# Keys and values of tile pairs in seven block products, and fp32 state and numerators on tiles of the array

## The chip, the core and the metric

The kernel runs on one core of one Trainium2 chip. The metric is the time of one execution on the device in microseconds (us). TensorE (PE) multiplies matrices into PSUM, ScalarE (ACT), VectorE (DVE) and GpSimd (POOL) do the elementwise work, and SyncE (SP) issues most transfers.

## The reference

One layer for 2048 tokens of width 512, all in fp32:

```python
xn = layernorm(x)
q, k, v = split(xn @ wqkv)                     # 32 heads of 16
pq = einsum("bhsd,hdf->bhsf", q, w_phi)        # the same for pk
phi_q = concat([softmax(pq), softmax(-pq)])    # 32 features a head; the same for phi_k
kv = einsum("bhsf,bhsd->bhfd", phi_k, v)       # the state
z = einsum("bhsf->bhf", phi_k)
num = einsum("bhqf,bhfd->bhqd", phi_q, kv)     # the numerators
den = einsum("bhqf,bhf->bhq", phi_q, z)[..., None] + 1e-6
s = reshape(num / den) @ wo
gate, up = xn @ W_gate, xn @ W_up              # 512 to 1376
g = silu((gate * (gate > 0) * up) @ W_down)
out = x + s * g
```

The state is summed over all tokens, so no numerator can be formed before the last token's keys and values are there.

## The kernel before

**Precision.** Large products run in the rounded format fp32r, one pass each. An operand is split into a high part (rounded copy, ScalarE) and a low part (the rest, VectorE or GpSimd), and a product takes three matmuls: low by high, high by low, high by high. `mm3` issues them. A matmul of plain fp32 operands appears in the trace as two records.

**Tile stage.** The tokens come as 16 tiles of 128, in an order (`order`) that alternates between two blocks of 512, so that tiles 2m and 2m+1 are the same columns of two blocks. For each tile: normalisation (`norm_stats`, `norm_scale`, `norm_apply`), four transposes into `pxT`, the high and low parts of the turned tile into `XT`, and for each pair the sums of blocks that a Strassen-Winograd scheme needs (`sums_x`, `sums_hi`, `sums_lo`; the slots of `XT` are A11, A12, A21, A22 and S1 to S4). The feed-forward part uses these sums: `gate_up` has seven block products instead of eight. Keys and values do not: `project` takes 12 matmuls of 512 columns for `pk` (keys, with `w_phi` folded into the weights) and 12 for `pv`, per tile. `query` takes 12 more per tile (`pq`) and stores the result. `exponents` subtracts maximum and minimum per head on VectorE, `exp_part` is on ScalarE, `features` normalises, `features_split` makes the features' high and low part (`phl`) and adds the features to `zacc` with an accumulating transfer on GpSimd's queue. `kv_products` takes 8 matmuls of 256 columns per tile into four banks (`pkv`): high and low part of the values by high and low part of the features.

**State.** `state` adds the parts, transposes 32 by 32 blocks, and builds `kvhl`, block-diagonal 128 by 128 weights in a high and a low part. `zB` holds the sums of the features.

**Feed-forward part.** Two halves of 1024 tokens. In each, 11 slices of 128 hidden columns: `gate_up` (7 blocks of 6 matmuls of 512 columns), and `down` for groups of slices (`py`). In the first half the weight slices are combined and split by `f_prep` and stored, in the second half they are reloaded (`f_reload`). Slices 2 and 3 (`AHEAD`) are prepared and stored during the tile stage already, and reloaded in the first half too. At the end of each half `out_tile` multiplies by `wo` (`pso`).

**Queries' back part.** Beside it, eight units (`UNITS`, each two tiles of 128 by 1024 features) go through `q_pair` (exponents, weights, normalisation) and then `q_back` or `q_back2`: transpose, a high part on ScalarE, a low part on VectorE or GpSimd, and products with `kvhl` into `pnum`: 16 matmuls of 256 columns (`q_back`, two units) or 8 of 512 (`q_back2`, six units). The result is stored in two parts to DRAM (`o_store`), one is loaded and the other added to it by an accumulating transfer (`o_sum`), and `o_split` prepares it for `wo`.

**Order.** The program order of each engine is the order of issue. A planner (`Clock`) keeps an estimate of each engine's time from a table of costs; side work (weight preparation, units, stores) is a set of generators that `pump` advances when their engine is estimated to be nearly free and their inputs ready. `finish` forces the rest. `START`, `LEAD`, `LATER` and `DOWNS` are due places set by hand. All operations are recorded at one line, L59, so groups of the profile are told apart by their tiles.

Of the kernel before, what the change touches and what calls it, by code (L numbers as in the profile page):

```python
# [28 lines left out]
B8, B4, B2 = 3, 8, 41  # L29
# [6 lines left out]
AHEAD = (2, 3)  # L36

LATER = 9
START = (12, 15)
# [3 lines left out]
A21, A22, A11, A12, S1, S2, S3, S4 = range(8)  # L43
# [19 lines left out]
class Clock:  # L63
# [21 lines left out]
    def issued(self, key, name, a, k):  # L85
# [9 lines left out]
        if key == "tensor":  # L95
            n = o.free_size()
            cost = max(n, 245) + 30
            if name == "matmul" and a[2].dtype == F32 and not k.get("is_transpose"):
                cost = n * 3 + 460
# [60 lines left out]
def layer_kernel(ctx: ExitStack, tc: tile.TileContext, x, wkT, wqT, wv, wo, wf, cst, out):  # L160
# [93 lines left out]
    mhalf = sb.tile([P, 96], F32, name="mhalf")[:, 0:1]  # L254
# [4 lines left out]
    def norm_stats(n):  # L259
        xt = X.pop(n)  # L260
        xn = u2((P, D), "xn")
        sm, ss, rs, bias = small(1, "lm"), small(1, "lv"), small(1, "lr"), small(1, "lb")
        nc.scalar.activation(xn, xt, AF.Copy, scale=-1.0 / D, accum_out=sm)
        nc.scalar.activation(xn, xt, AF.Square, bias=sm, accum_out=ss)
        XN[n] = xn, xt, bias, rs, sm, ss

    def norm_scale(n):
        xn, xt, bias, rs, sm, ss = XN[n]
        nc.vector.tensor_scalar(rs, ss, 1.0 / D, 1e-5, op0=ALU.mult, op1=ALU.add)
        nc.gpsimd.tensor_tensor(rs, rs, mhalf, op=ALU.pow)  # L270

    def norm_apply(n):
        xn, xt, bias, rs, sm, ss = XN[n]
        nc.vector.tensor_scalar(bias, sm, rs, None, op0=ALU.mult)
        nc.scalar.activation(xn, xt, AF.Identity, bias=bias, scale=rs)
        XN[n] = xn

    def norm_vector(n):

        xt = X.pop(n)  # L280
        st, mv, rs = small(6, "bs", 2), small(2, "bm", 2), small(1, "br", 2)
        nc.vector.bn_stats(st, xt)
        nc.vector.bn_aggr(mv, st)
        nc.vector.tensor_scalar(rs, mv[:, 1:2], 1e-5, None, op0=ALU.add)
        nc.gpsimd.tensor_tensor(rs, rs, mhalf, op=ALU.pow)
        XN[n] = u2((P, D), "xn"), xt, mv, rs

    def norm_vector_apply(n):
        xn, xt, mv, rs = XN[n]
        for c in [slice(0, 256), slice(256, D)] if n == 0 else [slice(0, D)]:  # L290
            nc.vector.tensor_scalar(xn[:, c], xt[:, c], mv[:, 0:1], rs, op0=ALU.subtract, op1=ALU.mult)
        XN[n] = xn
# [27 lines left out]
    def turn(m, full=True):  # L320
        p = transpose_x(m)
        hi_xt(m, p)
        if full:
            full_xt(m, p)
        return m, p

    def sums_x(n):

        x0, x1 = XF.pop(n - 1), XF.pop(n)
        sa, sb_ = u2((P, 2, 2, P), "sa"), u2((P, 2, 2, P), "sb")  # L330
        add(nc.gpsimd, sa[:, 0], x1[:, 0], x1[:, 1])
        add(nc.gpsimd, sb_[:, 0], x0[:, 0], x1[:, 0], ALU.subtract)
        add(nc.gpsimd, sa[:, 1], sa[:, 0], x0[:, 0], ALU.subtract)
        add(nc.gpsimd, sb_[:, 1], x0[:, 1], sa[:, 1], ALU.subtract)
        SF[n] = sa, sb_

    def sums_hi(n):
        for s, c in zip(SF[n], (S1, S3)):
            nc.scalar.activation(XT[:, c:c + 2, 0, :, cols(n)], s, AF.Copy)

    def sums_lo(n):
        for s, c in zip(SF.pop(n), (S1, S3)):
            add(nc.gpsimd, XT[:, c:c + 2, 1, :, cols(n)], s, f32(XT[:, c:c + 2, 0, :, cols(n)]), ALU.subtract)
# [62 lines left out]

    def features(n, e, raised, pv, between):

        vhl = u4((P, H, 2, DH), "vhl", F32R)
        pvg = pv.rearrange("p (h f) -> p h f", f=DH)  # L410
# [3 lines left out]
        nc.scalar.activation(vhl[:, :, 0, :], pvg, AF.Copy)  # L414
# [3 lines left out]
        add(nc.vector, vhl[:, :, 1, :], pvg, f32(vhl[:, :, 0, :]), ALU.subtract)  # L418
        nc.vector.tensor_reduce(sm, groups(e), op=ALU.add, axis=AX.X)
        nc.vector.reciprocal(pv[:, 0:64], sm)  # L420
        VH[n] = vhl
        if n:
            features_scale(n, e, pv)

    def features_scale(n, e, pv):
        phi = e if n else zacc
        nc.vector.tensor_tensor(groups(phi), groups(e), pv[:, 0:64].unsqueeze(2).to_broadcast([P, 64, DH]), op=ALU.mult)
        EK[n] = phi

    def features_split(n):  # L430
        phi = EK.pop(n)
        phl = u8((P, NG, 2, P), "phl", F32R)
        split(phl[:, :, 0, :], phl[:, :, 1, :], flat(phi).rearrange("p (g f) -> p g f", g=NG), nc.gpsimd)
        if n:
            nc.gpsimd.dma_start(zacc, phi, accum_op=ALU.add)
        PHI[n] = phl

    def kv_products(n):
        phl, vhl = PHI.pop(n), VH.pop(n)
        if n == 0:  # L440
            PKV.extend(ps((P, 2, 256), name="pkv") for _ in range(NG // 2))
# [15 lines left out]
    def f_load(f):  # L457
        if f == AHEAD[-1]:
# [21 lines left out]
    def f_prep(f, keep=True):  # L480
# [20 lines left out]
        yield "gpsimd", wa[0]  # L501
        for c in range(2):
            add(nc.gpsimd, wa[1][:, c], rg[c][:, :, 0, :], f32(wa[0][:, c]), ALU.subtract)
# [5 lines left out]
        yield "gpsimd", wb[0]  # L509
        add(nc.gpsimd, wb[1], ta, f32(wb[0]), ALU.subtract)  # L510
# [4 lines left out]
        yield "gpsimd", wc[0]  # L515
        add(nc.gpsimd, wc[1], tb, f32(wc[0]), ALU.subtract)
# [8 lines left out]
        yield "gpsimd", fd[0]  # L525
        add(nc.gpsimd, fd[1], rd, f32(fd[0]), ALU.subtract)
# [180 lines left out]
    def q_pair(u):  # L707
# [87 lines left out]
        BACK[u] = pace.add((q_back if parts[0][0] == parts[1][0] else q_back2)(u, es, ez), first=True)  # L795
# [11 lines left out]
    def od(q):  # L807

        if q not in OD:
            OD[q] = dram((P, 4, 256), f"od{q}"), dram((P, 4, 256), f"ol{q}")  # L810
        return OD[q]

    def turned_parts(u, es, ez, j, pieces):

        th, tl = u4((P, 1024), "pTh", F32R), u4((P, 1024), "pTl", F32R)
        n = 1024 // len(pieces)

        a = 2 if len(pieces) == 2 else 1
        hi, lo = (t.rearrange("p (a t x) -> p t a x", a=a, x=32) for t in (th, tl))

        def blocks(t):
            return t.rearrange("p (t a x) -> p t a x", a=a, x=32)
        if UNITS[u][0][0] in QUERIES[0]:

            ez[j] = None
            for i in range(2):
                e, k = pieces[i * len(pieces) // 2]
                k += i * 512 % n
                et, c = ps(name="peT"), slice(16 // a * i, 16 // a * (i + 1))
                yield "vector", e  # L830
                nc.vector.transpose(et, flat(e)[:, k:k + 512])
                yield "scalar", et
                nc.scalar.activation(hi[:, c], blocks(et), AF.Copy)
                yield "vector", th
                add(nc.vector, lo[:, c], blocks(et), f32(hi[:, c]), ALU.subtract)
        else:
            et = ez[j]
            for i, (e, k) in enumerate(pieces):
                yield "vector", e
                nc.vector.transpose(et[:, i * n:(i + 1) * n], flat(e)[:, k:k + n])  # L840
            yield "scalar", et
            nc.scalar.activation(hi, blocks(et), AF.Copy)
            yield "gpsimd", th
            add(nc.gpsimd, lo, blocks(et), f32(hi), ALU.subtract)
        DONE_Q[u] += 1
        return th, tl

    def q_back(u, es, ez):

        (q, _), _ = UNITS[u]  # L850
        for j in range(2):
            th, tl = yield from turned_parts(u, es, ez, j, [(es[j], 0)])
            ez[j] = None
            yield "tensor", tl
            os_ = flat(es[j]).rearrange("p (a s t) -> p a s t", a=2, s=2)
            vh, vl = (t.rearrange("p (d t a x) -> p d a t x", d=2, a=2, x=32) for t in (th, tl))
            for a in range(2):
                p = ps((P, 2, 256), name="pnum")
                for s in range(2):
                    g = 4 * a + 2 * j + s  # L860
                    o = p[:, s, :].rearrange("p (t x) -> p t x", x=32)
                    mm(o, kvhl[:, 1, g, :], vh[:, s, a], s == 0, False)
                    mm(o, kvhl[:, 0, g, :], vl[:, s, a], False, True)
                nc.scalar.activation(os_[:, a], p, AF.Copy)
            es[j] = None
            del th, tl, vh, vl
            DONE_Q[u] += 1
            STORES[u].append(pace.when(os_, lambda j=j, os_=os_: [o_store(q, j, s, os_[:, :, s, :]) for s in range(2)]))
        yield None,

    def q_back2(u, es, ez):

        (q0, j), (q1, _) = UNITS[u]
        for s in range(2):
            th, tl = yield from turned_parts(u, es, ez, s, [(e, 512 * s) for e in es])
            if s:
                es[:] = [None] * 2
            yield "tensor", tl
            os_ = u4((P, 1024), "os") if ez[s] is None else ez[s]
            ez[s] = None  # L880
            os_ = os_.rearrange("p (a q t) -> p a q t", a=2, q=2)
# [499 lines left out]
```

## Time and profile before

| | |
|---|---|
| Median of 3 runs | 563.15 us (562.89 to 563.59) |
| The profiled execution | 562.88 us, span 561.1 us |
| Records of matmuls | 2618 |
| Mean granted TensorE clock | 1.0 |
| DMA | 137.98 MB, mean 246 GB/s |

The span runs from the first to the last instruction of the core. A matmul's busy time (0.389 us for 512 columns) overlaps that of its neighbours, so durations of a piece of the stream are read from the chain of work that ended last, where each piece lasts until the next begins.

### The profile page before, as it was taken

How to read it: one execution, taken by the hardware profiler on the slowest of the kernel's cores; microseconds unless marked ns; L12 is line 12 of the kernel's file. 1: busy time of each engine (PE TensorE's matmuls, PEld its weight loads, DVE VectorE, ACT ScalarE, POOL GpSimd, SP SyncE). 2: the span in 40 equal slices, each digit the busy share in tenths (PEclk: the TensorE clock that was granted, in tenths of full speed). 3: DMA queues.
4: the chain of work that ended last, by engine and by line, in shares of the span. 5: the costliest groups of instructions: out<-in, count | busy, mean ns of one | idle time of the engine just before them, and what ended most of it. 6: DMA issues, size and time to landing. Idle time of an engine off the chain costs nothing.

```text
span 561.1 us, 8197 instructions
## 1 busy us (share of the span) xinstructions
PE 555.5 (99%) x2618; PEld 465.0 (83%) x2618; DVE 386.2 (69%) x584; ACT 303.1 (54%) x543; POOL 404.6 (72%) x347
## 2 busy tenths in 40 slices
PE   8999999999999999999999999999999999999997
PEld 8888888888888888888888888887888888888886
DVE  5978777676657897799963432799883948665323
ACT  3898687765555557456464151235465555644510
POOL 1689987899888487997978333473568786888473
PEclk9999999999999999999999999999999999999999
DMA  8358999855599817979779999991755765559874
GB/s 285 132 157 238 269 270 324 245 153 166 150 304 321 313 61 261 356 266 285 269 250 322 331 388 410 370 396 47 202 187 193 244 206 183 157 179 320 252 210 165
DMA packets 84539, 137.98 MB, mean 246 GB/s; under 512 B 7824, under 2 KB 34320, under 8 KB 83600
## 3 DMA queue, kind: packets, MB, share of 16 engines
q1 hardware_dynamic: 81040, 125.33, 64.7%
q0 software_dynamic: 3312, 12.06, 11.1%
q8 instruction: 21, 0.34, 0.2%
q14 instruction: 22, 0.18, 0.1%
q10 hardware_dynamic: 144, 0.07, 0.0%
HBM read 76.87 MB, written 52.69 MB: 231 GB/s over the span
## 4 chain that ended last, share of the span: by engine, by line
PE 93%; DVE 3%; DMA 2%; issue 0%; SPq 0%; POOL 0%
PE py L59 21%; PE pd L59 10%; PE pa L59 9%; PE pb L59 8%; PE pv L59 8%; PE pk L59 8%; PE pq L59 8%; PE pso L59 8%; PE pc L59 6%; PE pkv L59 3%; PE pnum L59 3%; PE pxT L59 1%; PE pfold L59 1%; DMA pql<-pq 1%; DMA wd<-ws 1%; DVE eq L59 1%
## 5 line engine op out<-in xcount | busy, mean ns | idle before, releaser
L59 PE MATMUL py<-fdh,hl 128*128 128x512 f32 x176 | 68.5, 389 | 0.0
L59 PE MATMUL py<-fdh,hh 128*128 128x512 f32 x176 | 68.5, 389 | 0.0
L59 PE MATMUL py<-fdl,hh 128*128 128x512 f32 x176 | 68.5, 389 | 0.0
L59 PE MATMUL pa<-XT,wa 128*128 128x512 f32 x264 | 67.0, 389 | 0.0
L59 PEld LDWEIGHTS pa<-XT,wa 128*128 128x128 f32 x264 | 49.6, 188 | 10.3
L59 DVE TENSOR_TENSOR y<-py,y 128x512 f32<-128x512 f32 x40 | 27.5, 689 | 36.5 <-PE py L59 36.5
L59 POOL TENSOR_TENSOR phl<-ek,phl 128x1024 fp32r<-128x1024 f32 x15 | 36.1, 2409 | 10.7 <-ACT phl L59 10.7
L59 PE MATMUL pv<-wvh,XT 128*128 128x512 f32 x128 | 43.5, 401 | 0.0
L59 PE MATMUL pk<-wkh,XT 128*128 128x512 f32 x128 | 42.4, 392 | 0.0
L59 POOL TENSOR_TENSOR ez<-eq,zB 128x1024 f32<-128x1024 f32 x16 | 38.5, 2415 | 4.4 <-ACT eq L59 2.0
L59 POOL TENSOR_TENSOR hl<-t,hh 128x512 fp32r<-128x512 f32 x16 | 20.8, 1298 | 27.3 <-ACT hh L59 26.3
L59 PE MATMUL pq<-XT,wqh 128*128 128x512 f32 (+1 forms) x144 | 40.3, 366 | 0.0
L59 PEld LDWEIGHTS py<-fdh,hh 128*128 128x128 f32 x176 | 33.0, 188 | 6.9
L59 PEld LDWEIGHTS py<-fdl,hh 128*128 128x128 f32 x176 | 33.0, 188 | 6.8
L59 PEld LDWEIGHTS py<-fdh,hl 128*128 128x128 f32 x176 | 33.0, 188 | 6.8
L59 POOL TENSOR_TENSOR y<-y,ys 128x512 f32<-128x512 f32 x24 | 30.9, 1291 | 9.6 <-ACT ys L59 9.6
L59 PE MATMUL pd<-XT,wd 128*128 128x512 f32 x132 | 33.8, 390 | 0.5 <-DVE t L59 0.5
L59 PE MATMUL pd<-XT,wc 128*128 128x512 f32 x132 | 33.8, 389 | 0.0
L59 POOL TENSOR_TENSOR ol<-of,oh 128x512 fp32r<-128x512 f32 (+1 forms) x13 | 20.2, 1596 | 18.9 <-ACT oh L59 18.9
L59 PE MATMUL pc<-XT,wb 128*128 128x512 f32 x132 | 33.7, 389 | 0.0
L59 PE MATMUL pb<-XT,wb 128*128 128x512 f32 x132 | 33.5, 389 | 0.0
L59 POOL TENSOR_TENSOR pTl<-ez,pTh 128x1024 fp32r<-128x1024 f32 x10 | 24.0, 2400 | 8.4 <-ACT pTh L59 8.4
(174 smaller groups left out, 1559.2 us busy)
## 6 DMA issues: line engine op xcount, KB each, us to landing
zacc<-ek POOLq DMA_DIRECT2D x15, 512.0 KB, 5.8
xts<-XT SPq DMA_DIRECT2D x4, 1792.0 KB
XT<-xts SPq DMA_DIRECT2D x7, 1024.0 KB, 20.4
wa<-ws SPq DMA_DIRECT2D x26, 256.0 KB, 3.2
wb<-ws SPq DMA_DIRECT2D x26, 256.0 KB, 4.8
wc<-ws SPq DMA_DIRECT2D x26, 256.0 KB, 5.1
ws<-wa SPq DMA_DIRECT2D x22, 256.0 KB, 4.0
ws<-wb SPq DMA_DIRECT2D x22, 256.0 KB, 4.2
```

The source lines that it names most:

```text
L59: return self.tc.keep_in_program_order(op(*a, **k))
```

## The change

It has three parts.

**Seven products.** From pair 3 on (`FIRST`), the keys and values of tiles 2m and 2m+1 are one product of 2 by 2 blocks, in seven blocks of 6 matmuls with the sums S1 to S4 of the tokens and combined weights `T`. `pair` replaces the loop over single tiles for m of 1 to 7. The combined weights are made in pairs 1 to 3 by 28 steps, placed by hand in `PLAN` (first letter: engine v, g or s; second: combine, high or low). The token sums are made by two differences on VectorE and two additions on GpSimd. The second tile's normalisation statistics go to VectorE from pair 3 on, and one of two feature scalings to GpSimd.

**fp32 on tiles of the array.** `kv_products` multiplies features and values unsplit, 16 matmuls of 64 columns on four 32-column strips, all into one bank. Numerators are 16 matmuls of 256 columns per unit on eight tiles of 64 rows by 32 columns (`q_back` for all units), with `kvt` as 32-column weights. `features_split` splits nothing any more, `turned_parts`, `q_back2`, `o_store` and `o_sum` go, and a unit is stored with two transfers.

**Moves.** `AHEAD` is empty: slices 2 and 3 are prepared in the first half like the others and not reloaded there. The planner's cost of a matmul with a tile position is half its columns.

```diff
-B8, B4, B2 = 3, 8, 41
+B8, B4, B2 = 3, 8, 40
-AHEAD = (2, 3)
-
-LATER = 9
-START = (12, 15)
+AHEAD = ()
+FIRST = 3
+PLAN = {(1, "sums"): "vc50 vc51", (1, "split a"): "gc00", (1, "end"): "gc01", (2, "start"): "vc10", (2, "split b"): "vc11 vc20 gc21", (2, "scaled"): "gc30", (2, "mid"): "sh20 sh21 gl20 sh00 sh01 sh11", (2, "split a"): "vl11", (2, "turned"): "vl00 vl01 vc31", (2, "end"): "sh10 gl10 gc40", (3, "start"): "gl21 gc41 sh30", (3, "split b"): "gl30", (3, "sums"): "sh31", (3, "mid"): "vl31"}
+
+START = (14, 15)
...
-            cost = max(n, 245) + 30
+            cost = n // 2 if k.get("tile_position") else max(n, 245) + 30
...
+    def sums_x(n, p):
+
+        a, b = XF.pop(n - 1), u2((P, 2, 2, P), "sb")
+        add(nc.vector, b[:, 0], a[:, 0], p[:, 0], ALU.subtract)
+        add(nc.vector, b[:, 1], p[:, 1], b[:, 0], ALU.subtract)
+        SF[n] = b, a
+
+    def sums_more(n):
+        b, a = SF[n]
+        add(nc.gpsimd, a[:, 0], a[:, 0], b[:, 1])
+        add(nc.gpsimd, a[:, 1], a[:, 1], b[:, 1], ALU.subtract)
...
     def features_split(n):
         phi = EK.pop(n)
-        phl = u8((P, NG, 2, P), "phl", F32R)
-        split(phl[:, :, 0, :], phl[:, :, 1, :], flat(phi).rearrange("p (g f) -> p g f", g=NG), nc.gpsimd)
         if n:
-            nc.gpsimd.dma_start(zacc, phi, accum_op=ALU.add)
-        PHI[n] = phl
+            nc.gpsimd.dma_start(zacc, flat(phi), accum_op=ALU.add)
+        else:
+            nc.sync.dma_start(zacc, flat(phi))
+        PHI[n] = phi
...
-        for g in range(NG):
-            mm(PKV[g // 2][:, g % 2, :], vhl[:, 4 * g:4 * g + 4], phl[:, g, :, :],
-               n == 0 and g % 2 == 0, n == N - 1 and g % 2 == 1)
+            PKV.append(ps((P, 8, 64), name="pkv"))
+        for j in range(4):
+            for c in range(4):
+                r = slice(32 * c, 32 * c + 32)
+                nc.tensor.matmul(PKV[0][r, j], v[:, c, j], phi[:, c, j], start=n == 0 and j == 0,
+                                 stop=n == N - 1, skip_group_check=True, tile_position=(0, 32 * c))
+        if n == 0:
+            mm(PKV[0].rearrange("p j x -> p (j x)")[:, 256:], noughts[:, :P], noughts, False, False)
...
     def q_back(u, es, ez):
 
...
+        for j in range(2):
+            for c in range(2):
+                yield "vector", es[j]
+                x_ = slice(512 * c, 512 * c + 512)
+                nc.vector.transpose(ez[j][:, x_], flat(es[j])[:, x_])
+            DONE_Q[u] += 1
+        yield "tensor", *ez
+        ps_ = [ps((P, 2, 256), name="pnum") for _ in range(2)]
+        for j in range(2):
+            et = ez[j].rearrange("p (d t a x) -> p d a t x", d=2, a=2, x=32)
             for a in range(2):
...
+                for d in range(2):
+                    to = slice(32 * (2 * a + d), 32 * (2 * a + d) + 32)
+                    for r in range(2):
+                        rr = slice(64 * r, 64 * r + 64)
+                        o = ps_[r][to, j, :].rearrange("p (t x) -> p t x", x=32)
+                        nc.tensor.matmul(o, kvt[rr, 4 * a + 2 * UNITS[u][j][1] + d, :], et[rr, d, a],
+                                         start=j == 0, stop=True, skip_group_check=True, tile_position=(64 * r, 32 * (2 * a + d)))
...
+    def pair(m):
+
+        n, c = 2 * m, cols(2 * m)
...
+        seven = m >= FIRST
+        py = ps(name="pk")
+        if seven:
+            block(py, A11, WK[:2], True)
+            px = ps(name="pk")
+            nc.scalar.activation(px, py, AF.Copy)
+        else:
+            mm3(py, xt_cols(n), rows(WK), range(KD))
+        if m > 1:
+            features_k(n - 1, *EB.pop(), engine=MULT[1])
+        t_steps(m, "start")
+        pz = ps(name="pv")
+        if seven:
+            block(pz, S1, T[0], True)
+            block(px, S2, T[1], False)
+            va = u2((P, D), "va")
+            nc.scalar.activation(va, px, AF.Copy)
+        else:
+            mm3(pz, xt_cols(n + 1), rows(WV), range(KD))
...
+        if seven:
+            block(py, A12, WK[2:], False)
+        ea = exponents(py)
+        if seven:
+            block(px, S3, T[2], False)
+            vb = u2((P, D), "vb")
+            nc.scalar.activation(vb, px, AF.Copy)
+            VH[n + 1] = u2((P, D), "v")
+            add(nc.vector, by_head(VH[n + 1], True), by_head(pz), by_head(vb))
...
+        kv_products(n - 2)
+        pace.pump()
+        at[0] = n + 1
+        if n + 3 < N:
+            t = turn(n + 3)
+        exp_all(ea)
...
+        if n + 3 < N:
+            turned(*t)
+            sums_more(n + 3)
+            sums_hi(n + 3, 0)
...
+        query(n - 1)
+        features_k(n, ea, py, engine=MULT[0])
+        if n + 3 < N:
+            sums_hi(n + 3, 1)
+            sums_lo(n + 3)
...
+        kv_products(n - 1)
+        pace.pump()
+        if seven:
+            block(px, A22, T[3], False)
+        else:
+            px = project(n + 1, WK, "pk")
+        eb = exponents(px)
+        if seven:
+            block(pz, S4, WV[2:], False)
+            VH[n] = u2((P, D), "v")
+            add(nc.vector, by_head(VH[n], True), by_head(pz), by_head(va))
+        else:
+            va = project(n, WV, "pv")
+        if n + 4 < N:
+            t = turn(n + 4)
...
```

More of the change, by code (lines that the diff above doesn't have):

```diff
@@ L508, in f_prep @@
         put(f, 4, wc[0])
-        yield "gpsimd", wb[0]
-        add(nc.gpsimd, wb[1], ta, f32(wb[0]), ALU.subtract)
+        yield from sums_of(wb[1], ta, f32(wb[0]), ALU.subtract, wb[0])
         put(f, 3, wb[1])
@@ L514, in f_prep @@
         nc.scalar.activation(wd[:, 0], b22, AF.Copy)
-        yield "gpsimd", wc[0]
-        add(nc.gpsimd, wc[1], tb, f32(wc[0]), ALU.subtract)
+        yield from sums_of(wc[1], tb, f32(wc[0]), ALU.subtract, wc[0])
         put(f, 5, wc[1])
@@ L524, in f_prep @@
         put(f, 6, wd)
-        yield "gpsimd", fd[0]
-        add(nc.gpsimd, fd[1], rd, f32(fd[0]), ALU.subtract)
+        yield from sums_of(fd[1], rd, f32(fd[0]), ALU.subtract, fd[0])
         put(f, 8, fd[1])
@@ L794, in q_pair @@
         DONE_Q[u], STORES[u] = 0, []
-        BACK[u] = pace.add((q_back if parts[0][0] == parts[1][0] else q_back2)(u, es, ez), first=True)
+        BACK[u] = pace.add(q_back(u, es, ez), first=True)
     BACK, DONE_Q, STORES = {}, {}, {}
@@ L809, in od @@
         if q not in OD:
-            OD[q] = dram((P, 4, 256), f"od{q}"), dram((P, 4, 256), f"ol{q}")
+            OD[q] = dram((P, 4, 256), f"od{q}")
         return OD[q]
[L813 to L846, printed above, removed]
@@ L895, in o_store @@
-    def o_store(q, j, s, t):
-        for part in range(2):
-            r = slice(0, 64) if s == part else slice(64, P)
-            to = slice(0, 64) if s == 0 else slice(64, P)
-            nc.sync.dma_start(od(q)[part][to, j:4:2, :], t[r])
+            for c in range(2):
[5 more added lines that the diff above has]
+        ps_ = [ps((P, 2, 256), name="pnum") for _ in range(2)]
@@ L1071, in layer_kernel, with sums_of, t_prep, four @@
     norm_vector_apply(3)
+    def sums_of(o, a, b, op=ALU.subtract, *need):
+        yield "gpsimd", *(need or (a, b))
+        add(nc.gpsimd, o, a, b, op)
+    T, STEPS = {}, []
+    def t_prep():
+        def four(name, whole, dt=F32R):
+            if whole:
+                t = u4((P, 2, D), name, dt)
+                return [t[:, k] for k in range(2)]
+            return [u2((P, D), name, dt) for k in range(2)]
+        raw = [even_first(wv_raw[:, k, :]) for k in range(KD)]
+        t3, t4, pairs = four("t3", False, F32), [], {}
+        def source(i, k):
+            return raw[k + 2 * i] if i < 2 else by_parity((t3, t4)[i - 2][k])
+        def combine(engine, k, i):
+            if i == 5:
+                add(engine, by_parity(t3[k]), raw[k + 2], raw[k], ALU.subtract)
+            elif i < 2:
+                add(engine, raw[k], raw[k], by_parity(f32(WK[k][i])), ALU.subtract)
+            elif i == 2:
+                add(engine, raw[k + 2], raw[k + 2], raw[k], ALU.subtract)
+            else:
+                if not t4:
+                    t4.extend(four("t4", False, F32))
+                o, (wh, wl) = t4[k], WK[k + 2]
+                if i == 3:
+                    add(engine, by_parity(o), by_parity(f32(wh)), raw[k + 2], ALU.subtract)
+                else:
+                    add(engine, o, o, f32(wl))
+        def hi(i, k):
+            if i not in pairs:
+                if i < 3:
+                    pairs[i] = list(zip(four(f"h{i}", not i), four(f"l{i}", not i)))
+                else:
+                    h = u8((P, 2, 2, D), "th", F32R)
+                    pairs[i] = [(h[:, 0, j], h[:, 1, j]) for j in range(2)]
+                T[i] = pairs[i]
+            nc.scalar.activation(by_parity(T[i][k][0]), source(i, k), AF.Copy)
+        def lo(engine, i, k):
+            add(engine, by_parity(T[i][k][1]), source(i, k), by_parity(f32(T[i][k][0])), ALU.subtract)
+        def step(what):
+            e, op, i, k = what
+            engine, i, k = {"v": nc.vector, "g": nc.gpsimd, "s": None}[e], int(i), int(k)
+            if op == "h":
+                hi(i, k)
+            elif op == "l":
+                lo(engine, i, k)
+            else:
+                combine(engine, k, i)
+        STEPS.append(step)
+    def t_steps(m, where):
+        for what in PLAN.get((m, where), "").split():
+            STEPS[0](what)
     def all_preps():
@@ L1152, in layer_kernel @@
+    EB, MULT = [], [nc.gpsimd, None]
+    for m in range(1, NP):
+        pair(m)
+    features_k(N - 1, *EB.pop())
+    features_split(N - 1)
+    kvacc, zB = [None] * 2
     one, ones = u2((P, P), "one"), u2((P, P), "ones", F32R)
```

331 lines of the change are left out of this document (163 added, 168 removed).

## The prediction

> **What bounds the kernel now.** I read the page's busy times and its chain that ended last first, then the table of stages, then the chain piece by piece.
>
> ```profile
> span 561.1 us, 8197 instructions
> PE 555.5 (99%) x2618; PEld 465.0 (83%) x2618; DVE 386.2 (69%) x584; ACT 303.1 (54%) x543; POOL 404.6 (72%) x347
> PE 93%; DVE 3%; DMA 2%; issue 0%; SPq 0%; POOL 0%
> PE pidle L59 <- DVE mhalf L59: 1.1, 1, 1.1
> PE pxT L59 <- DVE xn L59: 0.5, 1, 0.5
> PE pd L59 <- DVE t L59: 0.5, 1, 0.5
> ```
>
> TensorE is busy for 555.5 of 561.1 us, and the three waits of the waits view for this engine add up to 2.1 us. No gap is left to win. A change can only shorten the stream of matmuls or open gaps in it. The same holds stage by stage (columns: window, its length, then busy time of PE, weight load, DVE, ACT, POOL):
>
> ```profile
> 64.00:103.00 39.00, 39.00 (x196) 32.85 (x195) 26.40 (x43) 28.88 (x57) 33.04 (x31) 1.00 1.02 295
> 103.00:166.00 63.00, 63.00 (x316) 53.53 (x315) 45.25 (x63) 37.97 (x67) 56.56 (x55) 1.00 0.68 195
> 166.00:354.00 188.00, 188.00 (x842) 156.09 (x841) 125.09 (x186) 91.82 (x172) 134.36 (x122) 1.00 0.85 297
> 354.00:530.00 176.00, 175.54 (x779) 144.53 (x778) 128.76 (x184) 89.52 (x142) 117.45 (x77) 1.00 0.70 224
> ```
>
> The first two rows are the stage of the 16 token tiles (keys, values, queries, state), the other two the two halves of the feed-forward part with the attention's queries beside it. TensorE fills each, at full clock (1.00). VectorE and GpSimd have slack everywhere, least in the tile stage, where GpSimd is busy for 56.6 of 63 us.
>
> A matmul's busy time overlaps its neighbours', so prices come from the chain, where a piece lasts until the next one begins (columns: start, length, what):
>
> ```profile
> 6.66 3.62 PE pfold L59 x32
> 67.25 0.95 PE pkv L59 x8
> 68.21 2.75 PE pk L59 x12
> 70.96 0.44 PE pxT L59 x4
> 71.39 2.77 PE pv L59 x12
> 74.17 2.72 PE pq L59 x12
> 214.71 0.91 PE pnum L59 x4
> ```
>
> From these rows: 0.229 us for a 512-column product of pk or pv (2.75 / 12), 0.227 for one of pq or pnum, 0.119 for a 256-column one of pkv, 0.110 for a transpose's record, and 0.113 for each record of pfold. Pfold is the only plain fp32 product in the stream that runs dense: each 128-column matmul appears as two records, so it costs 0.226 us, against 0.119 for twice the columns in the rounded format.
>
> **The change part by part.**
>
> *Seven products.* For pairs 2m, 2m+1 with m from 3 to 7, keys and values take 7 blocks of 6 matmuls in place of 4 projections of 12. That is 42 for 48, so 6 x 5 = 30 matmuls of 0.229 us go: **-6.9 us**, all of it on the path.
>
> *State products.* Before, a tile takes 8 matmuls of 256 columns, 0.95 us, and 16 tiles take 15.2 us. After, it takes 16 fp32 matmuls of 64 columns on four 32-column strips of the array, two records each, so 32 records. Nothing in the trace runs on a strip. Bounds: half of pfold's record is 0.0565 us for 64 columns; with four strips at once 32 records take 8 x 0.0565 = 0.45 us, one after the other 1.8 us, and if no record starts sooner than pxT's 0.110 after the last, 3.5 us. Over 16 tiles that is 7.2, 28.9 or 56.3 us. I take 0.90 us a tile, 14.4 in all, two strips at once: neighbouring matmuls lie on different strips, but the pieces are short and the two records of one matmul share a strip. **-0.8 us**, bounds -8.0 and +41.1.
>
> *Numerators.* Before, six units take 8 matmuls of 512 columns (1.82 us), two take 16 of 256 (1.90 us): 14.7 us. After, each unit takes 16 fp32 matmuls of 256 columns on tiles of 64 rows and 32 columns, 32 records of 2 x 0.113 = 0.226 us. Eight tiles at once: 4 deep, 0.90 us; one after the other 7.2 us. Over 8 units: 7.2 or 57.9. The loop goes over all eight tiles before it comes back to one, and the two row halves write different banks, so I take the lower end and a fifth on top, 1.1 us: 8.8. **-5.9 us**, bounds -7.5 and +43.2.
>
> *Changing the array's layout.* There are 16 + 8 = 24 bursts on strips, each entered and left, so 48 changes. Before has none. The nearest rows:
>
> ```profile
> L59 PE MATMUL pkv<-phl,vhl 128*128 128x256 f32 x128 | 17.7, 282 | 0.0
> L59 PE MATMUL pxT<-ident,xn 128*128 128x128 f32 x64 | 9.6, 273 | 0.5 <-DVE xn L59 0.5
> ```
>
> A pkv record lasts 0.282 us, but the next starts after 0.119: 0.163 us lies under the neighbours. A change costs between nothing and that, 48 x 0.163 = 7.8 us. I take half, **+3.9 us**. A gain has no reason here.
>
> The Trainium skill, TensorEngine Tiling (Array Packing), section Tiling Modes, states that a change of the tiling mode drains the engine. By it the term would be the whole 7.8 and the forecast 559.6; no run so far shows a change of layout. It has a rival of its own below.
>
> *VectorE in the tile stage.* One pair of tiles of before, 87.45 to 106.60 us:
>
> ```profile
> L59 DVE TENSOR_REDUCE mx<-pk 128x32 f32<-128x512 f32 x4 | 2.6, 686 | 2.5 <-PE pk L59 2.5
> L59 DVE TENSOR_TENSOR ek<-ek,pv 128x1024 f32<-128x1024 f32 x2 | 2.4, 1220 | 0.1
> L59 DVE TENSOR_REDUCE sm<-ek 128x64 f32<-128x1024 f32 x2 | 2.4, 1207 | 0.0
> L59 DVE TENSOR_TENSOR vhl<-pv,vhl 128x512 fp32r<-128x512 f32 x2 | 1.4, 692 | 1.3 <-ACT vhl L59 1.3
> L59 DVE TENSOR_TENSOR ek<-pk,mx 128x512 f32<-128x512 f32 x2 | 1.4, 686 | 1.8 <-DMA zacc<-ek 1.8
> L59 DVE TENSOR_TENSOR XT<-pxT,XT 128x512 fp32r<-128x512 f32 x2 | 1.4, 682 | 0.0
> L59 DVE TENSOR_TENSOR ek<-mx,pk 128x512 f32<-128x512 f32 x2 | 1.4, 676 | 0.0
> L59 DVE RECIPROCAL pv<-sm 128x64 f32<-128x64 f32 x2 | 1.1, 560 | 0.1
> L59 DVE TENSOR_SCALAR lb<-lm,lr 128x1 f32<-128x1 f32 x2 | 0.4, 206 | 0.0
> L59 DVE TENSOR_SCALAR lr<-lv 128x1 f32<-128x1 f32 x2 | 0.3, 142 | 0.0
> ```
>
> They add up to 14.4 us. After, one of the two 1.22 us scalings goes to GpSimd; the low part of the values goes (-1.4) and two additions that finish the values come (+1.4); two half-size differences of the tokens (an estimate of 0.4 each, above half of 0.69) and one set of batch statistics (an estimate of 0.9) come: about 14.9 us. TensorE needs 42 x 0.229 + 24 x 0.227 + 8 x 0.110 + 2 x 0.9 = 17.7 us per pair, where it needed 48 x 0.229 + 24 x 0.227 + 0.88 + 1.9 = 19.2. VectorE goes from 75 to 84% of the pair. It still fits. The order is stiff, however: the sums S1 and S3 of the next pair pass transpose, ScalarE, VectorE (queued behind the four operations of the exponents), GpSimd, ScalarE and GpSimd before the second block of that pair can start. Cover is about one query, one state burst, two blocks and one transposition, 2.7 + 0.9 + 2.8 + 0.4 = 6.8 us, and up to 9.5 with the other query. I take 0.3 us of waiting per pair for five pairs: **+1.5 us**, bounds 0 and 10 (2 us a pair, three of the operations above late).
>
> *ScalarE and GpSimd.* GpSimd's work in the tile stage and in the preparation of a weight slice:
>
> ```profile
> L59 POOL TENSOR_TENSOR phl<-ek,phl 128x1024 fp32r<-128x1024 f32 x15 | 36.1, 2409 | 10.7 <-ACT phl L59 10.7
> L59 POOL TENSOR_TENSOR XT<-sa,XT 128x512 fp32r<-128x512 f32 x8 | 12.4, 1548 | 0.0
> L59 POOL TENSOR_TENSOR tab<-rawg,tab 128x256 f32<-128x256 f32 x8 | 6.9, 868 | 0.3
> L59 POOL TENSOR_TENSOR wa<-rawg,wa 128x256 fp32r<-128x256 f32 x6 | 4.6, 821 | 0.0
> ```
>
> The feature split (36 us) goes, half of it returns as scaling, and the token sums shrink from four additions to two. In exchange 10 of the new weight combinations and splits come onto GpSimd (10 x 1.55 = 15.5 us, in pairs 1 to 3). Their other 18 steps go to VectorE and ScalarE. GpSimd ends below its present load there.
>
> The preparation of slices 2 and 3 moves out of the tile stage into the first half. A slice takes 4 x 0.87 + 2 x 0.82 + 3 x 1.55 + 1.0 = 10.8 us of GpSimd, so 21.6 us move into a window where it is busy for 134 of 188. On average that fits, and the 18 reloads of the two slices on SP's queue go with it, as do 48 of 64 numerator stores and the eight adding transfers on GpSimd's queue. But slice 2 is then prepared while slice 1 is multiplied, 42 x 0.227 = 9.5 us, and GpSimd needs 10.8 plus 2.6 for that slice's own splits. The waiting instruction would be a matmul of slice 2 on its last weights, with all of TensorE's queue behind it. **+1.0 us**, bounds 0 and 4 (13.4 less 9.5).
>
> The numerators' high and low parts, their copies and additions go from ScalarE, VectorE and GpSimd; TensorE waits for none of them now, so this is worth nothing. The start, the output products and the tail after the last matmul stay.
>
> **Sum.** -6.9 - 0.8 - 5.9 + 3.9 + 1.5 + 1.0 = -7.2 us. The profiled execution took 562.9 us (span 561.1 and 1.8 around it), 0.3 below the median of 563.15. So 562.9 - 7.2 = **555.7 us**.
>
> **The rivals.**
>
> *Two records of a matmul hold up the next tile (slower).* The two records of an fp32 matmul use the same tile, and pfold's start 0.113 apart without overlap. If matmuls start only in program order, the second record waits for the first, and every tile behind it waits too. Then overlap is two deep at most: a matmul costs one record. The state stays at 0.90 us, but a unit's numerators take 16 x 0.226 = 3.6 us, 28.9 in all, +14.2 in place of -5.9. The sum is +12.9: **575.8 us**. It decides from 2.0 us a unit on (14.7 + 1.3 over 8 units), where the sum passes zero. For it: the order written (both records together). Against it: eight tiles share nothing. Chance 0.18.
>
> The Trainium skill, TensorE: Matmul & The Clock Gate, Part 3, states that matmuls start and end strictly in program order. That is this rival's condition; its speedups are for one record per matmul, and no row here has tiles.
>
> *Every change of layout costs the whole pipeline.* 48 x 0.163 = 7.8 in place of 3.9: **559.6 us**. The section on Tiling Modes is its rule. For it: the overlap of 0.163 is there to be lost. Against it: loads for the next layout may run ahead. Chance 0.12.
>
> *VectorE paces the tile stage.* If the chain of sums comes 2 us late in each of five pairs and slice 2 waits 4 us, waits cost 14 in place of 2.5 and the sum is +4.3: **567.2 us**. For it: 84% busy in a stiff order. Against it: 6.8 us of cover. Chance 0.10.
>
> **How the numbers follow.** The forecast has 0.60, with a range of its own from 548 (state and numerators near four and eight at once, changes at 1 us, no waits) to 561. No difference that can be measured means within 0.2%, 1.1 us, which lies between the forecast's upper end and the third rival: 0.04. Faster by more: 0.57 of the forecast and 0.11 of the layout rival, 0.68. Slower by more: the other two rivals, 0.28. For 8 in 10 the range runs from 547 to 575: it leaves out most of the first rival above its time, and the lower bounds taken all together.
>
> **What would show it.** Right: 42 products of pk and pv in the chain per pair; a state burst of 0.7 to 1.2 us and a numerator burst of 0.9 to 1.5 us from its first record to the next product; TensorE at 98% or more; no waits above 3 us for the sums. The forecast is wrong if a numerator burst is over 2.0 us, if the record after a burst starts 0.3 us late, or if TensorE waits for XT or wd by more than 5 us in sum.

## The result and the profile after

The changed kernel took 562.6 us (median of 20 runs, 559.38 to 565.41) against 563.32 us (562.83 to 564.01) for the kernel before: a ratio of 0.9986, with a 95% interval of 0.9973 to 0.9998. The forecast was 555.7 us. That is a gain of 0.1%, where 1.3% was forecast. Its profiled execution took 562.98 us, 0.1 more than that of before. The runs after spread over 6 us, those of before over 1.2 us; the two fastest of the runs after had a mean granted clock of 0.995 and 0.997, the five slowest 0.987.

The lines of the page that answer to those of before, and TensorE's waits:

```profile
span 561.2 us, 9072 instructions
PE 548.0 (98%) x3149; PEld 444.8 (79%) x3149; DVE 383.3 (68%) x588; ACT 263.6 (47%) x467; POOL 347.9 (62%) x309
PE 77%; POOL 8%; DVE 5%; DMA 5%; issue 4%; ACT 0%; SPq 0%; POOLq 0%; DVEq 0%; ACTq 0%
PE pz L60 <- POOL zl L60: 3.4, 1, 3.4
PE pv L60 <- DVE l L60: 2.5, 1, 2.5
PE pd L60 <- DVE t L60: 1.2, 1, 1.2
PE pk L60 <- ACT pk L60: 1.0, 1, 1.0
```

TensorE's share of the chain fell from 93 to 77%, and GpSimd, which had none, has 8%. These four add up to 8.1 us, and all of them to 9.4, where all of before's came to 2.1. The wait at pd comes at 218 us. The windows show that the others lie in two short places, and that the granted clock falls there (columns: window, its length, PE busy, granted clock, DMA share, GB/s):

```profile
64.00:80.00 16.00, 12.40 (x45) 0.84 0.71 197
74.78:81.60 6.82, 6.40 (x14) 0.50 0.21 59
170.00:190.00 20.00, 16.57 (x95) 0.91 0.73 236
103.00:150.00 47.00, 47.00 (x360) 1.00 0.52 126
```

From 103 us on, where the seven products run pair after pair, TensorE is full at clock 1.00. The first place is the start of pair 3, the first with seven products, where the clock is halved from 74.78 to 81.60 us (second row); the second is the first half's second slice. In the stream of TensorE the first one looks like this (start, length, operation; the wait in brackets):

```profile
69.82 0.39 PE L60 MATMUL pv<-h,XT 128*128 128x512 f32 x1
72.74 0.47 PE L60 MATMUL pv<-l,XT 128*128 128x512 f32 x1 [2.53 <-DVE l L60]
75.12 0.79 PE L60 MATMUL pk<-h,XT 128*128 128x512 f32 x1 [0.98 <-ACT pk L60]
77.87 0.63 PE L60 MATMUL pk<-h,XT 128*128 128x512 f32 x1
78.30 0.63 PE L60 MATMUL pk<-wkh,XT 128*128 128x512 f32 x1
```

After the second wait matmuls start 0.43 us apart in place of 0.23, without waiting for anything: the granted clock is 0.50 there. Added over all starts from 69.82 to 81.3 us, what lies above the normal distances is 7.3 us, of which 3.5 are waits by the view of waits. At pz it is 5.2 us (3.4 of wait, the rest at half the clock), at pd 1.3.

**What held up the weights' low part.** VectorE and GpSimd at the same time:

```profile
64.70 4.91 DVE L60 TENSOR_TENSOR l<-wvr,h 128x512 fp32r<-128x512 f32 x1 [3.54 <-POOL l L60]
69.53 1.27 DVE L60 TENSOR_REDUCE mx<-pk 128x32 f32<-128x512 f32 x2
71.92 1.28 DVE L60 TENSOR_TENSOR l<-wvr,h 128x512 fp32r<-128x512 f32 x2
...
64.38 2.17 POOL L60 TENSOR_TENSOR ek<-ek,rc 128x1024 f32<-128x1024 f32 x1
66.28 1.53 POOL L60 TENSOR_TENSOR XT<-sb,XT 128x512 fp32r<-128x512 f32 x1
67.52 1.53 POOL L60 TENSOR_TENSOR XT<-xf,XT 128x512 fp32r<-128x512 f32 x1
```

The step vl11 (on VectorE, the low part of a block of combined weights) took 4.91 us. The two like it (vl00 and vl01, the third row) took 1.28 together. It began just after GpSimd had begun a chain of three operations without a gap, and ended 0.56 us after the last of them (69.05). Behind it, in order, stood the exponents and vl00, vl01, for which the second block of pair 3 waited. The last product of the exponents' pk ended at 62.7 us, and they began at 69.53: 2.0 us of that is vl11's own wait for GpSimd before it began (part of the 3.54 in the bracket of the first row), 4.2 its standing still, the rest its normal length.

**What held up pz.** The last addition of features to zacc, and what follows it:

```profile
166.94 10.07 DMA zacc<-ek
178.23 2.35 POOL L60 TENSOR_TENSOR zl<-zacc,zh 128x1024 fp32r<-128x1024 f32 x1 [7.18 <-ACT zh L60]
180.63 0.80 PE L60 MATMUL pz<-zl,ones 128*128 128x512 f32 x1 [3.43 <-POOL zl L60]
```

The same addition and the same operation in the kernel before:

```profile
zacc<-ek POOLq DMA_DIRECT2D x1, 512.0 KB, 5.7
174.06 2.41 POOL L59 TENSOR_TENSOR zl<-zacc,zh 128x1024 fp32r<-128x1024 f32 x1 [0.19 <-ACT zh L59]
```

The transfer took 10 us, beside the stores of the slices. The planner reckons with 8000 cycles, 3.3 us, and had put pz into TensorE's order at 177. Before, the addition was issued at 167.1 too, took 5.7 us beside stores as well, and zl began at 174.06 and ended 3.9 us ahead of pz at 180.3. So the wait has two halves: zl ended 4.1 us later than before, and TensorE came to pz 3.3 us earlier.

**The bursts on tiles.** One of each, with a neighbour on either side:

```profile
99.82 0.39 PE L60 MATMUL pk<-h,XT 128*128 128x512 f32 x1
100.14 0.65 PE L60 MATMUL pkv<-ek,v 128*32 128x64 f32 x32
100.73 0.66 PE L60 MATMUL pxT<-ident,xt 128*128 128x128 f32 x4
...
392.78 0.39 PE L60 MATMUL py<-fdh,hh 128*128 128x512 f32 x1
393.10 1.09 PE L60 MATMUL pnum<-ez,kvt 64*32 64x256 f32 x32
394.12 0.73 PE L60 MATMUL pa<-XT,wa 128*128 128x512 f32 x2
```

From the first record to the next product it is 0.59 and 1.02 us. The burst begins 0.32 after its predecessor, 0.09 over the normal 0.23, and the first product after it takes 0.11 longer (0.73 for two in place of 0.62). So a state burst costs 0.78 us, a numerator burst 1.22, where before they cost 0.95 and 1.82. In the single starts the 32 records come in groups: state, eight groups of four with 0.006 to 0.007 us between starts and 0.056 from group to group (0.080 after the first); numerators, four groups of eight with 0.240 and then 0.216 from one to the next. Those are four and eight tiles at once.

### The profile page after: what moved, and what is told of

The parts are those of the page before. It is cut to its first block, busy times and chain, and to the rows that moved or that the text cites. A ratio compares the mean times of both kernels' runs of the same rounds, so it can differ in the third digit from the quotient of the medians.

```text
span 561.2 us, 9072 instructions
## 1 busy us (share of the span) xinstructions
PE 548.0 (98%) x3149; PEld 444.8 (79%) x3149; DVE 383.3 (68%) x588; ACT 263.6 (47%) x467; POOL 347.9 (62%) x309
## 4 chain that ended last, share of the span: by engine, by line
PE 77%; POOL 8%; DVE 5%; DMA 5%; issue 4%; ACT 0%; SPq 0%; POOLq 0%; DVEq 0%; ACTq 0%
PE py L60 18%; PE pk L60 9%; PE pd L60 8%; PE pa L60 8%; PE pso L60 8%; PE pq L60 7%; PE pb L60 7%; PE pc L60 4%; PE pv L60 4%; DMA zacc<-ek 2%; DMA wvr<-wv 2%; PE pkv L60 2%; POOL tab L60 1%; PE pnum L60 1%; POOL ez L60 1%
## 5 line engine op out<-in xcount | busy, mean ns | idle before, releaser
L60 ACT ACTIVATE hh<-t 128x512 fp32r<-128x512 f32 x16 | 10.1, 632 | 56.3 <-DVE t L60 53.0
L60 DVE TENSOR_REDUCE mx<-pk 128x32 f32<-128x512 f32 x32 | 20.6, 684 | 18.8 <-PE pk L60 18.8
L60 PE MATMUL pk<-wkh,XT 128*128 128x512 f32 x88 | 31.1, 405 | 0.0
L60 PEld LDWEIGHTS pd<-XT,wd 128*128 128x128 f32 x132 | 24.5, 188 | 7.7 <-POOL wd L60 1.6
```

The lines of the kernel that those rows point to most:

```text
L60: return self.tc.keep_in_program_order(op(*a, **k))
```

## Experiments

Theories: **L**, the VectorE operation with two inputs in SBUF stands still while GpSimd's chain runs, and the weights come late; **Z**, pz is put into the order before zacc can have landed. Rivals: **V**, VectorE and the chain of sums pace the pairs; **G**, GpSimd has too much to do with slices 1 and 2.

**The low part later.**

```diff
-(2, "split a"): "vl11", (2, "turned"): "vl00 vl01 vc31"
+(2, "turned"): "vl00 vl01 vl11 vc31"
```

> The changed kernel with one step moved: the low part vl11 goes from behind the features of pair 2 to behind vl00 and vl01. Theory L: this VectorE operation has both inputs in SBUF and stood still for 4.2 us (4.908 us against 0.677 for its like) while GpSimd ran one operation after the other, and held up the exponents and vl00, vl01 behind it; the first wait of pair 3 (2.7 us) and the slow matmuls after it (4.6 us over their normal length, with the wait for pk) go, the time falls by 5 to 7 us to 556 to 558, and what remains of vl00's wait is under 1 us. Rival V: VectorE has too much to do in pair 2 in any order; moving one 0.68 us step leaves the wait over 2 us and the time within 1 us of the changed kernel's 562.6.

Measured: 560.39 us, ratio 0.9945 (0.9932 to 0.9958). Of the 7.3 us lost at pair 3, 3.6 are left, and none of that is vl00's: that step now stood still itself, but the exponents were ahead of it.

```profile
63.84 0.68 DVE L60 TENSOR_TENSOR ek<-mx,pk 128x512 f32<-128x512 f32 x1
L60 DVE TENSOR_TENSOR l<-wvr,h x3: 677/679/4418, 64.4 to 69.4; 128x512 fp32r<-128x512 f32 x3
63.63 2.17 POOL L60 TENSOR_TENSOR ek<-ek,rc 128x1024 f32<-128x1024 f32 x1
66.79 1.50 POOL L60 TENSOR_TENSOR XT<-xf,XT 128x512 fp32r<-128x512 f32 x1
PE pz L60 <- POOL zl L60: 5.1, 1, 5.1
```

The operation on pk at 63.84, which has one input in PSUM, ran at full speed beside GpSimd's 63.63. Vl00, right behind it, took 4.418 us and ended 0.56 after GpSimd (68.85 and 68.29). The time fell by 2.2 and not by 5 to 7, because TensorE reached pz earlier and waited 5.1 us there instead of 3.4. With the matmuls at half speed behind it, that place cost 7.9 us in place of 5.2: most of the gain was given back.

**The landing reckoned with.**

```diff
-            self.ready[o.name] = start + self.LANDING
+            self.ready[o.name] = start + (self.LANDING if key == "sync" else 24000)
```

> The changed kernel with the planner's estimate for a transfer from GpSimd's queue raised from 8000 to 24000 cycles of TensorE (3.3 to 10 us), which is what the last addition to zacc took (issued 166.94, landed 177.01). Theory Z: the matmuls of pz were put into TensorE's order before that transfer could have landed; they now come later, the wait of 3.6 us and the slow matmuls behind it (1.7 us) go, and the time falls by 4 to 5 us to 558. Rival G: GpSimd is too busy with slices 1 and 2 to make zl; then pz or the first products of slice 2 wait in the new order too, and the time falls by under 2 us.

Measured: 556.14 us, 0.9877 (0.9864 to 0.9889), 6.5 below the changed kernel: 5.2 of pz, and the wait at pd fell too. TensorE waits neither for zl nor for a weight of slice 2. The products of pz now stand later in its order, and zl was made from 198.6 us on:

```profile
L60 PE MATMUL pz<-zl,ones x2: 389/389/389, 201.9 to 202.4; 128*128 128x512 f32 x2
```

Z holds; G falls. Vl11 took 4.910 us again.

**Both.**

> Both edits of the two runs above. If L and Z are right and independent: 5 to 7 and 4 to 5 us off, 551 to 553. If one of the waits only moves (V or G): 556 to 559.

Measured: 553.71 us, 0.9828 (0.9816 to 0.9841). That is just above the 551 to 553 of L and Z. The pair-3 edit is worth 2.4 us here and not 5 to 7, with 3.5 us of other late steps left at pair 3.

**A reduction in vl11's place.**

```diff
+        if m == 2:
+            nc.vector.tensor_reduce(small(32, "probe", 1), wv_raw[:, 3, :].rearrange("p (h f) -> p h f", f=DH), op=ALU.max, axis=AX.X)
         t_steps(m, "split a")
```

> As the run with the low part later, but with a VectorE maximum over 128x512 with one SBUF input, whose result nobody reads, in the place from which vl11 was taken. Theory L (two SBUF inputs against GpSimd's reads): it takes 0.65 to 0.75 us although GpSimd's chain runs beside it. Rival S (VectorE stands still at that place whatever it runs: instruction loading, a semaphore, the spill of XT issued at 64.97): it takes 4 us or more.

```profile
60.56 0.68 DVE L60 TENSOR_REDUCE probe<-wvr 128x32 f32<-128x512 f32 x1
64.57 5.73 DVE L60 TENSOR_TENSOR l<-wvr,h 128x512 fp32r<-128x512 f32 x3
59.98 1.55 POOL L60 TENSOR_TENSOR t<-wkh,wvr 128x512 f32<-128x512 f32 x1
```

0.68 us, beside an operation of GpSimd. It ran earlier than vl11 had, for it did not have to wait for data from GpSimd, so it does not by itself exclude that VectorE stops beside the chain whatever it runs. (One run: 557.53 us.) These lines of the strip-by-strip run below do:

```profile
67.31 0.68 DVE L60 TENSOR_TENSOR ek<-mx,pk 128x512 f32<-128x512 f32 x1
L60 DVE TENSOR_TENSOR l<-wvr,h x3: 677/678/1340, 67.9 to 69.8; 128x512 fp32r<-128x512 f32 x3
67.17 1.52 POOL L60 TENSOR_TENSOR XT<-xf,XT 128x512 fp32r<-128x512 f32 x1
```

There the exponents' operations, which have at most one input in SBUF, ran beside GpSimd's chain (64.03 to 68.69) at their normal length. Only vl00, which came when the chain had 0.78 us left, stood still: it took 1.340 us and ended 0.56 after the chain.

**No seven products.** The second edit, and `FIRST = 99`, an empty `PLAN`, no `t_prep()`.

> The kernel of e2 (later landing) with no seven products: every pair takes the four projections of 12 matmuls, and the 28 weight steps are left out. Theory L/T (the whole loss at pair 3 comes from the weight steps): both the 30 saved matmuls (+6.9 us) and the 7.0 us lost at pair 3 go, so the time stays within 1 us of e2's 556.1. Rival V (VectorE and the chain of sums pace the pairs, whatever the weights cost): waits stay in the tile stage without the weight steps, and the time is 558 or more or has PE waits of over 2 us between 65 and 150 us.

Measured: 556.13 us, 0.9875 (0.9859 to 0.989), against 556.14 with them. Without the weight steps TensorE is full from 64 to 160 us:

```profile
PE 549.1 (99%) x3179; PEld 447.8 (81%) x3179; DVE 364.4 (66%) x568; ACT 255.9 (46%) x454; POOL 334.9 (60%) x299
64.00:103.00 39.00, 39.00 (x298) 31.41 (x297) 26.26 (x48) 19.70 (x34) 18.38 (x18) 1.00 0.73 196
103.00:160.00 57.00, 57.00 (x431) 45.77 (x430) 34.19 (x50) 25.42 (x44) 31.56 (x33) 1.00 0.57 155
```

The 30 more records (3179 for 3149) cost what the weight steps cost, as L has it. By what it expects here V falls, but this run alone is a weak test of it: without seven products no product of keys or values waits for the sums. The window from 103 to 150 us of the changed kernel is the better one, for there the sums are needed and TensorE is full. The parts other than the seven products, with the landing mended, are worth 7.3 us by themselves (563.42 to 556.13).

**Strip by strip.** Both edits, and the loops of `kv_products` exchanged (`for c` outside `for j`).

> The kernel of e3 (both edits) with the state's 16 matmuls in another order: four in a row on one strip, then the next strip; before, neighbours lay on different strips. Theory C (a strip takes its records one after the other, different strips run at once, and matmuls start in program order): a burst of 0.435 us from the first record to the last grows towards 32 x 0.0565 = 1.8 us, and 16 bursts cost up to 21 us more (575). Rival D (strips have queues of their own, order is of no matter): the bursts stay within 0.1 us and the time at 553 to 555.

```profile
97.68 1.39 PE L60 MATMUL pkv<-ek,v 128*32 128x64 f32 x32
99.00 0.66 PE L60 MATMUL pxT<-ident,xt 128*128 128x128 f32 x4
```

A burst lasts 1.32 us to the next product in place of 0.59, and the one run took 561.83. Records on one strip start 0.056 us apart, one after the other, so order matters and D is wrong. The 16 longer bursts make 11.7 us; the run is 8.1 above that of both edits, whose late steps at pair 3 no longer show (no wait above 0.3 us there). But 1.18 us from first to last record is less than 1.8: in the middle two strips alternate at 0.026 to 0.030. C is too strict; some of the next strip's records start before the present strip is done.

**GpSimd's chain shorter.**

```diff
-        features_k(n, ea, py, engine=MULT[0])
+        features_k(n, ea, py, engine=None if m == 2 else MULT[0])
```

> The kernel of e3 with the scaling of the features of tile 4 (2.17 us on GpSimd, first of three operations in a row) moved to VectorE (1.22 us). Theory L: vl00 is freed when GpSimd's chain ends; the chain ends about 2 us earlier and vl00 takes about 2 us less than its 4.28. The time falls by 0 to 1 us, as the wait that vl00 itself caused is gone already. Rival S: vl00 takes as long as before.

Measured: 551.22 us, 0.9783 (0.9769 to 0.9796), more than expected: the steps behind on VectorE and GpSimd came earlier as well, and the waits left at pair 3 fell with them.

```profile
L60 DVE TENSOR_TENSOR l<-wvr,h x3: 677/680/2727, 64.3 to 67.6; 128x512 fp32r<-128x512 f32 x3
65.00 1.50 POOL L60 TENSOR_TENSOR XT<-xf,XT 128x512 fp32r<-128x512 f32 x1
```

Vl00 began at 64.33 (64.92 in the kernel of both edits) and took 2.727 us in place of 4.28. It ended at 67.06, again 0.56 after GpSimd's last operation (66.50). The stall follows the chain's end and not the place; S falls.

**From pair 4 on.** The kernel of both edits with `FIRST = 4`.

> The kernel of e3 with the seven products from pair 4 on, the weight steps where they were. Six more matmuls (+1.4 us), and the three waits left at pair 3 (together 3.5 us lost) have a pair of 17 us more to end: 553.7 + 1.4 - 3.5 = 551.6, if L and T are all of it. If the waits move to pair 4 (V), 555.

Measured: 559.26 us, 0.9926 (0.9914 to 0.9939): a miss.

```profile
PE pv L60 <- POOL XT L60: 5.3, 1, 5.3
79.84 1.28 POOL L60 TENSOR_TENSOR l<-wvr,h 128x512 fp32r<-128x512 f32 x1 [10.44 <-DMA pq<-pqs]
87.61 1.81 POOL L60 TENSOR_TENSOR xf<-xf,sb 128x256 f32<-128x256 f32 x2
```

The waits did move to pair 4, as the rival had it, but VectorE was not the cause: the low part gl10 waited at the head of GpSimd's queue until a query's store landed (3.1 us in flight) and its buffer came free, and the token sums stood behind it. That buffers of that size are short in pair 3 is a reading of this wait; no run has more of them. Behind the wait the clock was halved for 6.8 us again: this place cost some 8 us.

**The last weights earlier, and the state in twos.** First `(3, "scaled"): "vl31"` for `(3, "mid"): "vl31"` on top of the shorter chain; then, on that, `kv_products(n - 2)` moved down beside `kv_products(n - 1)`.

> The kernel of e7 with the step vl31 (low part of the last combined weights) moved from behind the token sums of pair 3 to ahead of them. There it waits for its high part (ready at 77.3 us) and not for a buffer that a query store frees (80.5). Theory T (what is left at pair 3 are late weight steps): the wait of 1.4 us at the block A22 goes, 551.2 less 1.2 to 1.5, 549.9. Rival V: VectorE is late with the sums instead and the time stays at 551.

Measured: 550.32 us, 0.9773 (0.976 to 0.9787); the wait at A22 is gone from the view of waits, and the median is 0.9 us lower, though the intervals of the two ratios overlap.

> The kernel of e9 with the state products of tiles 2m-2 and 2m-1 next to each other, so that 7 of the 16 bursts lose their entry and exit. Theory M (a burst costs 0.46 us of records and 0.33 us for entering and leaving the strips, so the price is per change of layout): 7 x 0.33 = 2.3 us less than e9, 547.6, and a double burst of 1.1 us in place of 2 x 0.78. Rival N (the 0.33 us belong to the records or their waits): no less than e9, and a double burst of 1.5 us.

Measured: 549.98 us, 0.9756 (0.9741 to 0.9771).

```profile
96.58 1.10 PE L60 MATMUL pkv<-ek,v 128*32 128x64 f32 x64
97.62 1.20 PE L60 MATMUL pk<-th,XT 128*128 128x512 f32 x4
PE pv L60 <- POOL XT L60: 0.7, 1, 0.7
```

A double burst takes 1.04 us to the next product, 1.24 with what its neighbours lose; two single ones take 1.56. So M holds: 0.33 us belong to entering and leaving. Of the expected 2.3 us only some 0.3 show, within the spread of the runs. About 1.4 us are lost at the starts of pairs 4, 5 and 7, where TensorE now comes earlier to the sums S1 than they do (the wait of 0.7 is pair 4's); here the sums begin to pace. Both versions beat both kernels. They are 5.8 and 6.2 us below the run without seven products (556.13), so most of the 6.9 us of that part shows once the weights come in time.

## Why the prediction was wrong

| Term (us) | forecast | found | how |
|---|---|---|---|
| seven products | -6.9 | -6.9 | 30 records fewer |
| state, records | -0.8 | -8.0 | 16 x 0.45 for 15.2: the lower bound |
| numerators, records | -5.9 | -7.5 | 8 x 0.90 for 14.7: the lower bound |
| changes of layout | +3.9 | +7.8 | 16 x 0.33 and 8 x 0.32: the upper bound |
| waits, tile stage | +1.5 | +7.3 | pair 3, half of it at a slow clock |
| waits, feed-forward part | +1.0 | +6.5 | 5.2 at pz, 1.3 at pd |

The sum found is -0.8, and +0.1 was measured between the two profiled executions; the 0.9 us between them are not assigned. The split of a burst into records and layout takes the records at their lower bound and calls the rest layout; the state in twos supports it.

**The matmuls** have the right sign and were too cautious: -9.7 forecast with the layout, -14.6 found. Three sizes were off. These 4.9 us hid part of the 11.3 us that the waits were forecast too small, so with better sizes here the forecast would have missed by more; that it came within 7 us is luck in part. The lower end of its range, 548, is loose too: the terms named for it, at their bounds, give 541.5. Tiles overlap as fully as the bounds allowed, so the rival of two records that hold up the next tile falls, though one matmul's two records share a tile. The changes of layout came out at the 7.8 of the rival in which each costs the whole pipeline. The Trainium skill, TensorEngine Tiling (Array Packing), section Tiling Modes, says that a change of mode drains the engine, and the trace agrees, with 0.33 us for a burst's two changes.

**The failed step is that of the waits.** It asked whether VectorE's 84% fits and how much cover the sums have. (The rows of VectorE add up to 14.8 us and not 14.4, so it is 86%.) The sums were in time: TensorE is full from 103 to 150 us, and its busy 98% came true as forecast, for matmuls at half speed count as busy. What was late was the preparation of the weights, which the prediction priced as busy time of three engines and gave no chain of its own. It added up that GpSimd "ends below its present load". But one 0.68 us step on VectorE waited out GpSimd's chain, 4.2 us, and in all ten kernels that have the weight steps the first low part to meet the chain ended 0.56 us after it. The kernel before has no such operation in this stage: its VectorE operations on two tensors there have one of them in PSUM. The Trainium skill, SBUF — State Buffer, section Who interferes with whom, says that a VectorE instruction with two SBUF inputs contends with a GpSimd instruction that reads SBUF. Its section SBUF: two separate sides says that whichever of the two starts first has the shared ports for its whole instruction. The trace agrees and goes further: VectorE's step got its turn only after three instructions of GpSimd in a row. That it is the ports is the account of the Trainium skill; the runs show which operations stand still, and until when.

**The second wait was not in the prediction at all.** It looked at GpSimd's 13.4 us against the 9.5 us of a slice; that was no wait in the run with the landing reckoned with. The last addition to zacc, which pz needs, has no term of its own there. TensorE came to pz 3.3 us earlier than before, and the addition, issued at the same time, landed 10 us after its issue in place of 5.7; together that used up the 3.9 us that zl had been early and 3.4 us more. Why the transfer took longer stays open. The planner's 3.3 us had been wrong before too, and the later pz hid it.

Third, the waits cost up to twice their length: 7.3 us for 3.5 at pair 3, 5.2 for 3.4 at pz. The prediction priced waits at their own length; after these the granted clock was 0.50 for 6.8 and 3.4 us.

## What to carry to other kernels

When a kernel is bound by one engine without gaps, a shorter stream can lay bare estimates and transfers that the old one covered; price the one-off preparations and the last transfer of a stage as chains with a due time, and not as busy time. Keep VectorE operations with both inputs in SBUF away from runs of GpSimd operations, or behind all that is urgent. Small matmuls on tiles of the array are worth the entry and exit of a burst, 0.33 us here, so put them next to each other; here that was worth 0.3 us of the 2.3 expected, as other waits took its place.

## What the hardware showed that was not expected

A VectorE operation of 0.68 us took 4.91, 4.42, 4.28, 2.73 and 1.34 us, always until 0.56 us after GpSimd's last of several operations without a gap. GpSimd's own operations there took 1.53 and 2.17 us, against 1.30 and 1.94 for the same ones from 88 us on; one at 63.13, before the stall, took 1.53 too, so the runs do not show that the stall is the reason. Plain fp32 matmuls, two records each, ran on eight tiles at once: 32 records of 256 columns in four groups 0.24 and then 0.216 us apart. Whether the second record of a matmul starts out of program order, or the program has the records of several matmuls interleaved, the runs do not show. The half-speed clock does not follow every gap: at pair 3, with 2.5 and 1.0 us of waiting and five matmuls between, it came in the changed kernel and again with the landing mended, but after 3.3 us of waiting at pz in the run with the reduction it did not. Where it came between 60 and 190 us it lasted 3.4 or 6.8 us; what decides that it comes, the runs do not show. An accumulating transfer of 512 KB took 10 us where stores of 256 KB beside it took 10 as well, and 5.7 us in the kernel before.
